# State products and scores in 64x32 tiles, w1 loaded by head pairs, and a new order of the work

## The chip, the core and the metric

The kernel runs on one core of one Trainium2 chip. The metric is the device time of one execution in microseconds (us), taken as the median of the runs. TensorE (PE) multiplies, with its weight loads shown apart (PEld); VectorE (DVE), ScalarE (ACT) and GpSimd (POOL) do the element work; SyncE (SP) issues most transfers (DMA).

## What is computed

Eight batches; in each, 512 rows of x in 8 heads of 64, and 32 state rows per head. Attention reads the state from x and x from the state; the 544 rows of 512 that result go through a normalized two-layer network with a hidden width of 2048.

```python
# B, H, S, Ns, D = 8, 8, 512, 32, 64
scores = x @ state^T / sqrt(D)                  # per batch and head
xread  = softmax(scores) @ state                # 512 rows
sread  = softmax(scores^T over x) @ x           # 32 rows
r   = concat([xread, sread], rows) -> (B, 544, 512)
rn  = (r - mean(r)) / sqrt(var(r) + 1e-6) * g_ln
out = r + relu(rn @ w_ch1) @ w_ch2              # w_ch1 512x2048, w_ch2 2048x512, both float64
```

## The kernel before

Numbers are held as a high and a low f16 part, and a product is made of three terms, high by high, high by low and low by high (`TERMS`). Heads are grouped as h = 4g + j, with g the half (0 or 1) and j the place in it (0 to 3); u is one of four units of 512 hidden columns, t, c and s are parts of the rows.

The weights come first. For each unit, `weights1` loads a float64 block of w1 in two transfers (L585), turns it to f32 on ACT and DVE (`words`), takes the column means off with f32 matmuls (L599), finds the largest value (L608), and splits the result into a high and a low part in the raw buffer. Four transfers inside SBUF (the last lines of `weights1`) then lay high and low of one head beside each other on the 128 partitions as `w1c`, so that one matmul with 128 rows makes two of the terms at once. `weights2` prepares w2 the same way without the rearrangement, and `sums_of_weights` makes the three weight sums that a Strassen form of the second product needs, by adding and subtracting 256-column blocks on PE with plus and minus the identity (L747).

Per batch, `attention` loads x and state, scales and splits them, transposes them by DMA, and computes the scores (L403): 32 state rows of one head against x, four heads side by side in 128x32 tiles of the PE array, 8 matmuls per g. After the softmax, `read_state` (L479) multiplies x by the numerators, and four f32 matmuls with a folded identity (L492) add the halves and turn the result. `state_products` (L665) multiplies each head's state rows by w1c, giving per unit and g a 128x512 block in a PSUM bank named `half`, with 8 matmuls in 128x32 tiles; ACT and DVE take it off as the high and low parts of `matrix`. Then `products` runs for each half batch and unit a first product (L799, from `matrix` and the softmax numerators `ea`) and a Strassen second product (L855, from `xs`, `w2h` and `sums`). Batch 0 has a plain form (L701 and L715). The state rows of all batches go through the network last (L808), with a second copy of the high halves of w1c, named `high`, that eight transfers make.

PSUM has 8 banks: four accumulators (`acc`), two `half`, and one pair named `banks`, which scores, read_state and the mix of L515 use in turn.

The order is written out by hand. Every step of every stream is a closure made by `do`; the text `PLAN` lists stream and step numbers, and `issue` calls them in this order. Each engine works through its own steps in that order, SP's transfers included, and a step waits for its inputs and for its buffer. `L186` is the line inside `do`, so nearly every element operation and transfer carries it and is told apart by its tiles.

## Time and profile before

| | |
|---|---|
| median of 3 runs | 668.11 us (667.76 to 668.94) |
| span of the profiled execution | 665.9 us |
| PE busy | 626.3 us (94%) |
| DVE busy | 498.0 us (75%) |
| ACT busy | 388.2 us (58%) |
| POOL busy | 216.7 us (33%) |
| bytes moved by DMA | 69.63 MB, mean 105 GB/s |

The span runs from the first to the last instruction of one profiled execution, whose own time is not given apart; the span lies 2.2 us below the median of the runs. A matmul's recorded duration is its latency: matmuls are pipelined, so what a row of n of them costs PE is read from the start of one row of the timeline to the start of the next.

### The profile page before, as it was taken

The page shows a single profiled execution, that of the slowest core. Times are in us where ns is not written, and L with a number is a line of the kernel's source. Part 1 is how long each engine was busy: PE and PEld are TensorE (multiplying, and loading weights), DVE is VectorE, ACT ScalarE, POOL GpSimd, SP SyncE. Part 2 cuts the span into 40 slices and gives each one's busy share as a digit, 9 for nine tenths or more (in the row PEclk, how much of TensorE's full clock was granted, in tenths as well). Part 3 has the DMA queues.
Part 4 walks back from the last instruction along what each step waited for, and adds up shares of the span by engine and source line. Part 5 has one row for each costly group of instructions (what it writes and reads, how often), then busy time and mean ns, then how long its engine had stood idle before and what let it go on. Part 6 is the DMA issues. An engine that isn't in the chain of part 4 may idle for free.

```text
span 665.9 us, 14680 instructions
## 1 busy us (share of the span) xinstructions
PE 626.3 (94%) x5948; PEld 493.1 (74%) x5948; DVE 498.0 (75%) x1002; ACT 388.2 (58%) x699; POOL 216.7 (33%) x189
## 2 busy tenths in 40 slices
PE   0676999999999999999999999999999999999996
PEld 0242755548887887788888888878778887888885
DVE  5989986697788677966887689777976897465533
ACT  5488989667546474547465756465546564344331
POOL 0000333321344325323452226433433343234222
PEclk9977999999999999999999999999999999999998
DMA  8999836924231534330516142305142311244221
GB/s 324 309 278 210 259 103 146 141 57 103 71 74 37 136 104 78 95 94 8 92 32 162 67 88 68 97 5 122 35 126 47 76 32 43 81 116 104 73 56 32
DMA packets 98563, 69.63 MB, mean 105 GB/s; under 512 B 72704, under 2 KB 90624, under 8 KB 98048
## 3 DMA queue, kind: packets, MB, share of 16 engines
q1 hardware_dynamic: 96384, 64.77, 37.5%
q0 software_dynamic: 864, 3.15, 2.6%
q8 instruction: 46, 0.75, 0.5%
q10 hardware_dynamic: 1248, 0.79, 0.4%
q14 instruction: 21, 0.17, 0.1%
HBM read 28.05 MB, written 9.44 MB: 56 GB/s over the span
## 4 chain that ended last, share of the span: by engine, by line
PE 90%; DVE 5%; DMA 2%; ACT 1%; issue 1%; DVEq 0%; SPq 0%
PE acc L855 41%; PE half L799 22%; PE acc L715 6%; PE half L665 5%; PE acc L701 3%; PE half L808 3%; PE acc L747 2%; PE acc L599 2%; PE banks L403 1%; DVE w_t L186 1%; PE banks L479 1%; PE banks L515 1%; PE banks L492 1%; DMA x_f<-in_x_dram 1%; PE acc L608 1%; DMA w1c<-raw 1%
## 5 line engine op out<-in xcount | busy, mean ns | idle before, releaser
L855 PEld LDWEIGHTS <-xs 128*128 128x128 f16 x2520 | 242.4, 98 | 43.6 <-issue 15.3
L186 POOL TENSOR_TENSOR xs<-rs,xs 128x512 f16<-128x512 f32 x120 | 142.4, 1199 | 272.7 <-ACT xs L186 207.1
L855 PE MATMUL acc<-w2h,xs 128*128 128x256 f16 x1440 | 183.0, 273 | 0.0
L799 PE MATMUL half<-ea,matrix 128*128 128x256 f16 x1344 | 159.4, 273 | 0.0
L799 PEld LDWEIGHTS <-matrix 128*128 128x128 f16 x1344 | 130.7, 98 | 16.6 <-issue 0.8
L855 PE MATMUL acc<-sums,xs 128*128 128x256 f16 x1080 | 141.9, 273 | 0.0
L186 DVE SCALAR_TENSOR_TENSOR rs<-half,rs 128x256 f32<-128x256 f32 x224 | 89.4, 419 | 27.6 <-ACT rs L186 13.3
L186 ACT ACTIVATE xs<-rs 128x512 f16<-128x512 f32 x128 | 77.1, 618 | 40.5 <-DVE rs L186 33.8
L186 ACT ACTIVATE xs<-half 128x256 f16<-128x256 f32 (+1 forms) x112 | 53.6, 487 | 72.5 <-PE half L799 50.5
L186 DVE SCALAR_TENSOR_TENSOR xs<-half,xs 128x256 f16<-128x256 f32 (+1 forms) x112 | 61.2, 550 | 28.1 <-ACT xs L186 24.5
L186 ACT ACTIVATE matrix<-half,hs 128x512 f16<-128x512 f32 x56 | 38.0, 687 | 35.2 <-PE half L665 34.9
L186 DVE SCALAR_TENSOR_TENSOR matrix<-half,hs,matrix 128x512 f16<-128x512 f32 x56 | 41.2, 742 | 16.0 <-ACT matrix L186 15.3
L186 ACT ACTIVATE rs<-half 128x256 f32<-128x256 f32 x56 | 21.3, 381 | 42.5 <-PE half L799 40.1
L715 PE MATMUL acc<-w2h,hid 128*128 128x512 f16 x192 | 43.1, 379 | 0.0
L186 DVE TENSOR_TENSOR strip<-acc,strip 128x256 f32<-128x256 f32 (+1 forms) x60 | 33.2, 554 | 10.5 <-PE acc L855 7.5
L665 PE MATMUL half<-w1c,sT 128*32 128x512 f16 x448 | 33.5, 384 | 1.9 <-DVE rs L186 1.0
L186 POOL TENSOR_TENSOR ts<-ts,mA 128x1024 f32<-128x1024 f32 (+1 forms) x8 | 14.4, 1804 | 60.9 <-DVE mA L186 54.5
L715 PEld LDWEIGHTS <-hid 128*128 128x128 f16 x192 | 18.5, 98 | 20.9 <-issue 0.4
L186 DVE SCALAR_TENSOR_TENSOR x<-x_f,x_s,x 128x512 f16<-128x512 f32 x32 | 24.8, 798 | 5.3 <-ACT x L186 5.3
L186 DVE BATCH_NORM_STATS2 s<-xr 128x6 f32<-128x512 f32 x32 | 21.6, 684 | 8.7 <-ACT xr L186 8.6
L186 ACT ACTIVATE x<-x_f,x_s 128x512 f16<-128x512 f32 x32 | 21.7, 713 | 9.8 <-DVE x_s L186 9.8
L186 POOL TENSOR_TENSOR hid<-strip,hid 128x512 f16<-128x512 f32 x16 | 18.5, 1170 | 26.6 <-ACT hid L186 26.5
(152 smaller groups left out, 770.1 us busy)
## 6 DMA issues: line engine op xcount, KB each, us to landing
raw<-in_moe_w_ch_dram SPq DMA_DIRECT2D x9, 1024.0 KB, 7.3
out_dram<-xr SPq DMA_DIRECT2D x16, 512.0 KB, 3.0
x_f<-in_x_dram SPq DMA_DIRECT2D x15, 512.0 KB, 5.6
sums<-in_moe_w_ch_dram SPq DMA_DIRECT2D x7, 1024.0 KB, 8.2
ek<-ea SPq DMA_DIRECT2D x56, 64.0 KB, 2.1
ek<-ek SPq DMA_DIRECT2D x7, 512.0 KB, 4.3
xr<-part POOLq DMA_DIRECT2D x6, 512.0 KB, 5.0
w1c<-raw SPq DMA_DIRECT2D x8, 256.0 KB, 5.1
```

The costliest lines, as they stand in the source:

```text
L186: return lambda: f(*map(now, args), **{k: now(v) for k, v in kw.items()})
L403: nc.tensor.matmul(o[32 * j:32 * j + 32], lhsT=sT[:, g, a, 32 * j:32 * j + 32], rhs=xT[:, s, 4 * g + j].rearrange("p c t -> p (c t)"), sta ...
L479: nc.tensor.matmul(ps_z[:, h // 4, :, h % 4], lhsT=xv[:, c // hc, h, c % hc], rhs=ebT[:, :, h // 4, c, 32 * (h % 4):32 * (h % 4) + 32], st ...
L492: nc.tensor.matmul(pr[:, g], lhsT=z4[:, g, i], rhs=fold, start=i == 0, stop=i == 1, skip_group_check=True)
L599: nc.tensor.matmul(ps, lhsT=gm[:, k:k + 1].broadcast_to([P, P]), rhs=t4[:, k], start=k == 0, stop=k == 3)
L665: nc.tensor.matmul(ps[32 * j:32 * j + 32], lhsT=sT[:, g, a, 32 * j:32 * j + 32], rhs=w[:, 2 * g + j // 2, j % 2], start=a == 0, stop=a == ...
L701: nc.tensor.matmul(o[:, 256 * f:256 * f + 256], lhsT=m[:, g, i, P * (q + f):P * (q + f) + P], rhs=ea[:, s, k, g], start=f == 0 and g == 0 ...
L715: nc.tensor.matmul(po, lhsT=hid[:, i, q, c * P:(c + 1) * P], rhs=w[:, j, q], start=first and q == 0 and n == 0, stop=last and q == 3 and n ...
L747: nc.tensor.matmul(o, lhsT=signs[:, k // 2], rhs=v[k], start=start and k == 0, stop=k == 3, skip_group_check=True)
L799: nc.tensor.matmul(ps[:, 256 * q:256 * q + 256], lhsT=m[:, h, i, P * (2 * k + q):P * (2 * k + q) + P], rhs=ea[:, 0, j, h, 256 * g:256 * g ...
L808: nc.tensor.matmul(ps[:, 256 * q:256 * q + 256].rearrange("p (t n) -> p t n", t=2), lhsT=w[:, k // 2, k % 2, fs] if k < H else wn[:, k - H ...
L855: nc.tensor.matmul(po[o], lhsT=y[:, n, i, o] if o < 2 else x[:, o - 2, n, i], rhs=v[j], start=u == 0 and n == 0 and k == 0 and o in (2, 1, ...
```

## The change

- **State products.** One step per unit makes both g. Each matmul has 64 rows and 32 columns of the array: g picks the upper or lower 64 rows, j the quarter of the columns. There are 24 per unit (three terms, four j, two g) where there were 16. From batch 1 on the results go to the two banks of `banks` and are taken off in one ACT and one DVE instruction of 2x512 columns; before, each g had its own `half` bank and its own pair of 512 columns.
- **Scores.** The same tiles: 24 matmuls in one step where two steps had 8 each.
- **w1.** It is loaded so that the partition is (g, row of the head) and the free index is (j, column), in four transfers per unit in place of two, and the split writes w1c directly. The 16 transfers of 256 KB inside SBUF and the eight that made `high` are gone. The gain vector and the state rows follow that layout, and L808 reads w1c alone with the same number of matmuls.
- **read_state.** The three terms apart: 48 matmuls of 64 columns where there were 32; the four f32 fold matmuls become one f32 transpose, after two copies of 64 rows, one on ACT and one on DVE.
- **Weight sums.** Full 512-column blocks; one bank is continued from sum to sum: 12 matmuls of 512 columns per unit where there were 32 of 256.
- **Batch 0** loads x in two halves by rows (pieces of 512 bytes) where it had halves by heads (1 KB).
- **Order.** `PLAN` is replaced as a whole:

```diff
-    "1:0 1:3-4 1:1-2 1:5-12 4:1 1:19 1:72 0:0 4:6 1:20 1:24-25 4:5 4:7 4:0 4:3 1:17-18 4:2 4:4 3:1 3:6 1:22-23 "
+    "0:0 1:1 1:0 1:2-3 1:5 1:4 1:6-8 4:1 1:9-11 1:71 1:12 1:18 1:21 4:6 1:19 1:22 1:13 4:0 1:16 1:23 1:17 2:0 4:3 "
...
+            o, i = (xf[:, hh], src[:, :, 2 * hh:2 * hh + 2]) if b == 0 else (xf[:, 0, hs], src[:, hs])
+            yield do(engines[hh].dma_start, out=o, in_=i)
...
-        def scores(s, g, o, sT, xT):
-            for a in range(2):
+        def scores(s, ps, sT, xT):
+            for n, (a, i) in enumerate(TERMS):
                 for j in range(4):
-                    nc.tensor.matmul(o[32 * j:32 * j + 32], lhsT=sT[:, g, a, 32 * j:32 * j + 32],
-                                     rhs=xT[:, s, 4 * g + j].rearrange("p c t -> p (c t)"),
-                                     start=a == 0, stop=a == 1, skip_group_check=True)
-
-        psv = ps if parts == 1 else ps.rearrange("p s (g t) -> p g s t", g=G)
-        eB = quad("eB").rearrange("p (g s t) -> p g s t", g=G, s=parts)
+                    for g in range(G):
+                        k = hc * (4 * s + j)
+                        nc.tensor.matmul(ps[32 * j:32 * j + 32, g, w * s:w * s + w],
+                                         lhsT=sT[D * g:D * g + D, a, 32 * j:32 * j + 32],
+                                         rhs=xT[D * g:D * g + D, k:k + hc, i], start=n == 0, stop=n == 2,
+                                         skip_group_check=True)
...
         def read_state(ps_z, x16, ebT):
-            xv = x16.rearrange("p (s h c) i d -> p s h c (i d)", s=parts, c=hc)
-            for h in range(H):
+            for j in range(4):
                 for c in range(C):
-                    nc.tensor.matmul(ps_z[:, h // 4, :, h % 4], lhsT=xv[:, c // hc, h, c % hc],
-                                     rhs=ebT[:, :, h // 4, c, 32 * (h % 4):32 * (h % 4) + 32],
-                                     start=c == 0, stop=c == C - 1, skip_group_check=True)
+                    a = hc * (4 * (c // hc) + j) + c % hc
+                    for n, (i, k) in enumerate(TERMS):
+                        nc.tensor.matmul(ps_z[:, j], lhsT=x16[:, a, i], rhs=ebT[:, k, :, c, 32 * j:32 * j + 32],
+                                         start=c == 0 and n == 0, stop=c == C - 1 and n == 2, skip_group_check=True)
         yield do(read_state, ps_z, x16, ebT)
-        z = halves("z").bitcast(F32)[:, 0:512]
-        z4 = z.rearrange("p (g i n) -> p g i n", g=G, i=2)
-        pr = pz[:, 1, 0:G * D].rearrange("p (g d) -> p g d", g=G)
+        z = halves("z").bitcast(F32)[:, 0:P]
+        pr = pz[:, 1, 0:G * D]
         sread = fixed([P, G, D], F32, "sread")
-        yield do(nc.scalar.activation, z, pz[:, 0], AF.Copy)
-
-        def fold_halves(pr, z4):
-            for g in range(G):
-                for i in range(2):
-                    nc.tensor.matmul(pr[:, g], lhsT=z4[:, g, i], rhs=fold, start=i == 0, stop=i == 1,
-                                     skip_group_check=True)
-        yield do(fold_halves, pr, z4)
-        yield do(nc.vector.tensor_tensor, sread, pr, rB.unsqueeze(2).broadcast_to([P, G, D]), ALU.mult)
+        for g, copy in enumerate((partial(nc.scalar.activation, func=AF.Copy), nc.vector.tensor_copy)):
+            r = slice(D * g, D * g + D)
+            yield do(copy, z[r].rearrange("p (j n) -> p j n", j=4), ps_z[r, :, g])
+        yield do(nc.tensor.transpose, pr, z, idf)
+        yield do(nc.vector.tensor_tensor, sread, pr.rearrange("p (g d) -> p g d", g=G),
+                 rB.unsqueeze(2).broadcast_to([P, G, D]), ALU.mult)
...
+            rows_of = w1[:, 1024 * u:1024 * u + 1024].rearrange("(g j d) f -> g d j f", g=G, j=4)
+            for k in range(2):
+                nc.sync.dma_start(out=raw[:, 1024 * k:1024 * k + 1024], in_=rows_of[:, :, 2 * fh + k])
...
-        hl = raws[1].bitcast(F16).rearrange("p (i e) -> p i e", i=2)
-        yield from split(hl[:, 0], hl[:, 1], t, scale)
-        hl = hl.rearrange("p i (k f) -> p i k f", k=4)
-        w = narrow(u, "w1c").bitcast(F16).rearrange("p (k s f) -> p k s f", k=4, s=2)
-        w1c[u] = w
-        for i in range(2):
-            for s in range(2):
-                to = 64 * (i ^ s)
-                yield do(nc.sync.dma_start, out=w[to:to + 64, :, s], in_=hl[64 * s:64 * s + 64, i])
+        w = narrow(u, "w1c").bitcast(F16).rearrange("p (i e) -> p i e", i=2)
+        yield from split(w[:, 0], w[:, 1], t, scale)
+        w1c[u] = w.rearrange("p i (j f) -> p i j f", j=4)
...
-        def multiply(ps, g, sT, w):
-            for a in range(2):
+        def multiply(ps0, ps1, sT, w):
+            for n, (a, i) in enumerate(TERMS):
                 for j in range(4):
-                    nc.tensor.matmul(ps[32 * j:32 * j + 32], lhsT=sT[:, g, a, 32 * j:32 * j + 32],
-                                     rhs=w[:, 2 * g + j // 2, j % 2], start=a == 0, stop=a == 1, skip_group_check=True)
+                    for g in range(G):
+                        nc.tensor.matmul((ps0, ps1)[g][32 * j:32 * j + 32],
+                                         lhsT=sT[D * g:D * g + D, a, 32 * j:32 * j + 32],
+                                         rhs=w[D * g:D * g + D, i, j], start=n == 0, stop=n == 2, skip_group_check=True)
         sT = results[b][1]
         for u in range(U):
             m = matrix[b][u] = block(4, f"matrix_{u}", 1, "matrix").bitcast(F16).rearrange("p (g i f) -> p g i f", g=G, i=2)
-            for g in range(G):
-                ps = accumulator() if b == 0 else half()
-                scale = CM if b == 0 else hs[:, u:u + 1]
-                yield do(multiply, ps, g, sT, w1c[u])
-                yield do(nc.scalar.activation, m[:, g, 0], ps, AF.Copy, scale=scale)
-                yield do(nc.vector.scalar_tensor_tensor, m[:, g, 1], ps, scale, m[:, g, 0], ALU.mult, ALU.subtract)
+            scale = CM if b == 0 else hs[:, u:u + 1]
+            if b == 0:
+                ps = [accumulator() for _ in range(G)]
+                todo = [(ps[g], m[:, g, 0], m[:, g, 1]) for g in range(G)]
+            else:
+                two = banks()
+                ps = [two[:, g] for g in range(G)]
+                todo = [(two, m[:, :, 0], m[:, :, 1])]
+            yield do(multiply, *ps, sT, w1c[u])
+            for v, hi, lo in todo:
+                yield do(nc.scalar.activation, hi, v, AF.Copy, scale=scale)
+                yield do(nc.vector.scalar_tensor_tensor, lo, v, scale, hi, ALU.mult, ALU.subtract)
...
+        def add(sign, first, last, ps, *v):
+            for i in range(2):
+                nc.tensor.matmul(ps, lhsT=signs[:, sign], rhs=v[i], start=first and i == 0, stop=last and i == 1,
                                  skip_group_check=True)
-        for n in range(2):
-            ps = [accumulator() for _ in range(2)]
-            (b21, b22), (b11, b12) = ([[w[:, i, n, k, 256 * x:256 * x + 256] for i in range(2)] for x in range(2)]
-                                      for k in range(2))
-            t3, t2, n4 = ([sums16[:, u, k, i, n] for i in range(2)] for k in range(3))
-            o = [v[:, 256 * x:256 * x + 256] for v in ps for x in range(2)]
-            for pairs in (((t3, b22, b12), (b12, b12, b11)), ((t2, b22, b12),), ((n4, b21, t2),)):
-                first = len(o)
-                def subtract_all(*v, first=first):
-                    for k in range(len(v) // 5):
-                        subtract(first != 1 and k == 0, *v[5 * k:5 * k + 5])
-                todo = [(d, a, b, o.pop(0)) for d, a, b in pairs]
-                yield do(subtract_all, *[v for d, a, b, p in todo for v in (p, *a, *b)])
-                for d, a, b, p in todo:
-                    yield do(nc.scalar.activation, d[0], p, AF.Copy)
-                    yield do(nc.vector.tensor_tensor, d[1], p, d[0], ALU.subtract)
+        def difference(ps, a0, a1, b0, b1):
+            add(0, True, False, ps, a0, a1)
+            add(1, False, True, ps, b0, b1)
+        (b21, b22), (b11, b12) = ([[w[:, i, :, k, 256 * x:256 * x + 256] for i in range(2)] for x in range(2)]
+                                  for k in range(2))
+        t3, t2, n4 = ([sums16[:, u, k, i] for i in range(2)] for k in range(3))
+        ps, pb = (accumulator().rearrange("p (n e) -> p n e", n=2) for _ in range(2))
+        yield do(difference, ps, *b22, *b12)
+        yield do(nc.scalar.activation, t3[0], ps, AF.Copy)
+        yield do(nc.vector.tensor_tensor, t3[1], ps, t3[0], ALU.subtract)
+        yield do(difference, pb, *b12, *b11)
+        yield do(add, 0, False, True, ps, *b11)
+        yield do(nc.scalar.activation, t2[0], ps, AF.Copy)
+        yield do(nc.vector.tensor_tensor, t2[1], ps, t2[0], ALU.subtract)
+        yield do(nc.scalar.activation, b12[0], pb, AF.Copy)
+        yield do(nc.vector.tensor_tensor, b12[1], pb, b12[0], ALU.subtract)
+        yield do(add, 1, False, True, ps, *b21)
+        yield do(nc.scalar.activation, n4[0], ps, AF.Copy, scale=-1.0)
+        yield do(nc.vector.scalar_tensor_tensor, n4[1], ps, -1.0, n4[0], ALU.mult, ALU.subtract)```

What the new order does is seen in the engines' rows. First SP's queue in the first 90 us, where the rearranging transfers stood (x_f and s_j are loads of a batch, ebT a transpose). Before:

```order
L186 DMA_TRANSPOSE ebT<-eb 128x16x128
L626 DMA raw<-in_moe_w_ch_dram 128x2x1024
L186 DMA w1c<-raw 64x4x512 x2
L186 DMA w1c<-sums 64x4x512
L186 DMA w1c<-raw 64x4x512 x6
L626 DMA raw<-in_moe_w_ch_dram 128x2x1024
L186 DMA w1c<-sums 64x4x512 x3
L186 DMA s_j<-in_state_dram 128x2x64
L626 DMA sums<-in_moe_w_ch_dram 128x2x1024
```

The same place with the change:

```order
L191 DMA x_f<-in_x_dram 128x4x256
L616 DMA raw<-in_moe_w_ch_dram 128x2x1024
L191 DMA_TRANSPOSE ebT<-eb 128x16x128
L616 DMA raw<-in_moe_w_ch_dram 128x2x1024
L191 DMA s_r<-in_state_dram 32x8x64
L191 DMA s_j<-in_state_dram 128x2x64
```

The loads of w2 (L626, now L616) follow one another with no w1c transfer between them.

Second, DVE in the same stretch, from the end of the first unit's w1 (its low part is written to `raw` before, to `w1c` now) to the first blocks of `matrix`. Before:

```order
L186 SCALAR_TENSOR_TENSOR raw<-w_t,of_weights,raw 128x2048 x2
L186 SCALAR_TENSOR_TENSOR w_t<-w_t,gx,acc 128x512 x4
L186 TENSOR_REDUCE dA<-ts 128x16
L186 TENSOR_SCALAR dA<-dA 128x16
L186 SCALAR_TENSOR_TENSOR sums<-w_t,of_weights,sums 128x2048
L186 RECIPROCAL dA<-dA 128x16
L186 SCALAR_TENSOR_TENSOR matrix<-acc,matrix 128x512
```

With the change:

```order
L191 STREAM_TRANSPOSE ef<-ts 128x512
L191 TENSOR_SCALAR of_weights<-of_weights 128x1
L191 SCALAR_TENSOR_TENSOR matrix<-acc,matrix 128x512
L191 TENSOR_SCALAR is_297<-of_weights 128x1
L191 RECIPROCAL of_weights<-is_297 128x1
L191 SCALAR_TENSOR_TENSOR w_t<-w_t,gx,acc 128x512
L191 SCALAR_TENSOR_TENSOR ea<-ef,ea 128x512
```

The first block of `matrix` now comes after the low part of one unit of w1, where three units' low parts stood ahead of it; the other units' follow later.

Third, DVE in the middle of the program, where a batch's state products are taken off between steps of the hidden blocks (`rs`, `xs`). Before:

```order
L186 SCALAR_TENSOR_TENSOR eb<-eB,eb 128x1024
L186 SCALAR_TENSOR_TENSOR matrix<-half,hs,matrix 128x512
L186 SCALAR_TENSOR_TENSOR xs<-half,xs 128x2x256
L186 TENSOR_REDUCE dA<-ts 128x32
L186 TENSOR_SCALAR dA<-dA 128x32
L186 RECIPROCAL dA<-dA 128x32
L186 SCALAR_TENSOR_TENSOR matrix<-half,hs,matrix 128x512 x2
```

With the change:

```order
L191 SCALAR_TENSOR_TENSOR ea<-ef,ea 128x1024
L191 SCALAR_TENSOR_TENSOR matrix<-banks,hs,matrix 128x2x512
L191 SCALAR_TENSOR_TENSOR xs<-half,xs 128x2x256
L191 SCALAR_TENSOR_TENSOR rs<-half,rs 128x256 x4
L191 SCALAR_TENSOR_TENSOR xs<-half,xs 128x2x128 x2
L191 SCALAR_TENSOR_TENSOR rs<-half,rs 128x256
L191 SCALAR_TENSOR_TENSOR matrix<-banks,hs,matrix 128x2x512
```

There are half as many take-offs, each of 2x512 columns, and other steps stand between them.

More of the change, by code (lines that the diff above doesn't have):

```diff
@@ L1 @@
 from contextlib import ExitStack
+from functools import partial
 import concourse.bass as bass
@@ L281, in load_batch @@
         engines = nc.sync, nc.sync if b > 0 else nc.scalar
-        xf = rows("x_f").rearrange("p (h c d) -> p h c d", h=H, c=C)
+        parts = 2 if b == 0 else 1
+        xf = rows("x_f").rearrange("p (s h c d) -> p s h c d", s=parts, h=H, c=C // parts)
         sj = fixed([P, G, D], F32, "s_j")
@@ L887, in products @@
             yield together()
-    high, state_rows_T = [None] * U, [None]
-    def high_halves(u):
-        high[u] = quad("high").bitcast(F16).rearrange("p (k f) -> p k f", k=4)
-        for s in range(2):
-            half = slice(64 * s, 64 * s + 64)
-            yield do(nc.sync.dma_start, out=high[u][half], in_=w1c[u][half, :, s])
+    state_rows_T = [None]
     def state_rows():
@@ L937, in moe_attention @@
         streams += these
-    streams += [list(state_rows()), *(list(high_halves(u)) for u in range(U))]
+    streams += [list(state_rows())]
     streams += [list(s) for s in products(B)]
```

108 lines of the change are left out of this document (50 added, 58 removed), and 242 rows, old and new, of the table PLAN.

## The prediction, made before the change was run

> **What bounds the kernel now.** I read the busy times by stage first, then what PE waited for after the start, then the chain that ended last. Columns of the first view: stretch, its length, busy time of each engine with its instructions, granted TensorE clock, DMA share, GB/s.
>
> ```profile
> core 0: us, PE busy (x) PEld busy (x) DVE busy (x) ACT busy (x) POOL busy (x), PEclk, DMA share, GB/s
> 0.00:81.00 81.00, 49.12 (x373) 27.06 (x373) 68.42 (x127) 57.53 (x80) 7.34 (x12) 0.87 0.93 274
> 81.00:660.00 579.00, 577.12 (x5583) 465.99 (x5575) 427.51 (x873) 330.68 (x620) 209.37 (x177) 1.00 0.34 81
> ```
> ```profile
> PE half L665 <- DVE rs L186: 1.0, 1, 1.0
> PE half L665 <- DVE xs L186: 0.9, 1, 0.9
> ```
> ```profile
> PE 90%; DVE 5%; DMA 2%; ACT 1%; issue 1%; DVEq 0%; SPq 0%
> ```
>
> From 81 to 660 us PE is busy 577 of 579 us at full clock, and its two waits there come to 1.9 us. DVE, the next engine, is busy 427.5 of 579 (74%). So after the start a microsecond of PE work is a microsecond of time, and work taken from DVE, ACT or DMA alone is worth nothing. Before 81 us DVE leads (68.4 of 81).
>
> **Prices on PE.** Counts of the parts that change, then rows of the timeline; the cost of a row is the distance to the next start.
>
> ```profile
> L665 PE MATMUL half<-w1c,sT 128*32 128x512 f16 x448 | 33.5, 384 | 1.9 <-DVE rs L186 1.0 <-DVE xs L186 0.9
> L403 PE MATMUL banks<-xT,sT 128*32 128x512 f16 x112 | 8.0, 382 | 0.0
> L479 PE MATMUL banks<-ebT,x 128*128 128x64 f16 x256 | 9.5, 199 | 0.0
> L492 PE MATMUL banks<-fold,z 128*128 128x64 f32 x64 | 8.2, 272 | 0.7 <-ACT z L186 0.7
> L747 PE MATMUL acc<-w2h,signs 128*128 128x256 f16 x112 | 15.4, 273 | 0.0
> L747 PE MATMUL acc<-sums,signs 128*128 128x256 f16 x16 | 3.1, 272 | 0.0
> ```
> ```profile
> 202.28 0.82 PE L855 MATMUL acc<-w2h,xs 128*128 128x256 f16 x6
> 203.03 0.62 PE L665 MATMUL half<-w1c,sT 128*32 128x512 f16 x8
> 203.58 1.48 PE L855 MATMUL acc<-w2h,xs 128*128 128x256 f16 x12
> 204.90 0.82 PE L855 MATMUL acc<-sums,xs 128*128 128x256 f16 x6
> ...
> 86.50 1.05 PE L665 MATMUL half<-w1c,sT 128*32 128x512 f16 x16
> 87.48 1.49 PE L701 MATMUL acc<-ea,matrix 128*128 128x256 f16 x12
> ...
> 140.64 7.93 PE L715 MATMUL acc<-w2h,hid 128*128 128x512 f16 x36
> 148.41 1.47 PE L747 MATMUL acc<-w2h,signs 128*128 128x256 f16 x12
> ...
> 157.36 1.10 PE L479 MATMUL banks<-ebT,x 128*128 128x64 f16 x32
> 158.29 1.47 PE L799 MATMUL half<-ea,matrix 128*128 128x256 f16 x12
> 159.60 1.00 PE L492 MATMUL banks<-fold,z 128*128 128x64 f32 x8
> 160.44 0.38 PE L747 MATMUL acc<-w2h,signs 128*128 128x256 f16 x2
> ...
> 241.64 0.27 PE L186 MATMUL banks<-idf,x_am 128*2 128x128 f32 x1
> 241.75 0.82 PE L855 MATMUL acc<-sums,xs 128*128 128x256 f16 x6
> ```
>
> A 256-column matmul costs 0.109 us (158.29 to 159.60, 12 of them); one of 512 columns 0.216 (140.64 to 148.41, 36). A group of 8 in 128x32 tiles begins 0.09 after the six before it are through (202.28 + 6 x 0.109 = 202.94, start 203.03) and holds PE 0.55: two waves of 0.216 and 0.12 more. So a lone group of 8 costs 0.64, and a group of 16 costs 0.98 + 0.09 = 1.07. How such a wave runs is seen in slices of 20 ns (the number in brackets after PE is how many matmuls are in flight, after PEld how many weight loads):
>
> ```profile
> 274.72:274.74 0.02, 0.02 (x4) 0.02 (x7) 0.02 (x1) 0.00 (x0) 0.00 (x0) 1.00 0.00 0
> 274.80:274.82 0.02, 0.02 (x4) 0.02 (x7) 0.02 (x1) 0.00 (x0) 0.00 (x0) 1.00 0.00 0
> 274.84:274.86 0.02, 0.02 (x4) 0.00 (x0) 0.02 (x2) 0.00 (x0) 0.00 (x0) 1.00 0.00 0
> 274.94:274.96 0.02, 0.02 (x8) 0.00 (x0) 0.02 (x1) 0.00 (x0) 0.00 (x0) 1.00 0.37 90
> ```
>
> Four matmuls start together, one per quarter; the weights of the next four are loaded by 274.84, under the first four; the next four start at 274.93, a streaming time later.
>
> **State products.** The changed group has 24 matmuls in eight tiles: three waves, if the two row halves run together, 0.09 + 3 x 0.216 + 0.12 = 0.86. Bound above, if the halves take turns: six waves, 1.51. No row shows two halves of 64 rows at once. The nearest is the 32-row tiles of L530:
>
> ```profile
> 43.52 0.96 PE L530 MATMUL acc<-sh,ea 32*128 32x64 f16 x34 [1.01 <-DVE ea L186]
> ```
>
> 34 of them start within about 0.76 us (0.96 less one latency, 0.20 as L479's row has it), 0.022 each, while 64 columns on the whole array cost 0.029 (0.93/32, 157.36 to 158.29). Calls on different row strips follow one another there, so strips do overlap somewhat. I take 0.86. By the Trainium skill, "TensorEngine Tiling (Array Packing)", section Tiling Modes, tiles operate independently and a change of mode drains the array; by it too the group has three waves, and the 0.09 and 0.12 above are such drains.
>
> Counting PE's rows from the first second product (L715) on, before has 46 lone groups of 8 and 5 of 16: 46 x 0.64 + 5 x 1.07 = 34.8 us. The change has 29 groups: 29 x 0.86 = 24.9. **Gain 9.9.** Scores there: 8 lone groups and 3 of 16, 8.3, against 7 groups, 6.0: **gain 2.3.**
>
> **Weight sums.** 128 x 0.109 = 14.0 against 48 x 0.216 = 10.4: **gain 3.6.** **read_state**, seven batches: 48 for 32 matmuls, 16 x 0.029 x 7: **loss 3.2.** **The fold**: 0.84 a batch (159.60 to 160.44), against one f32 transpose. A transpose with a two-column weight costs 0.11; a full f32 weight costs about as much to load again (the fold's eight records are 0.105 apart with only 64 columns each). I take 0.21, between 0.11 and 0.42: 7 x 0.63, **gain 4.4** (2.9 to 5.1). One more group of 12 of L701 stands ahead of L715: **gain 1.3.** Sum of the dense part: 9.9 + 2.3 + 3.6 - 3.2 + 4.4 + 1.3 = 18.3 us.
>
> **The shared bank pair.** State products now use `banks`. Its take-off has no row of 2x512 columns from PSUM with both parts; the nearest are
>
> ```profile
> L186 ACT ACTIVATE xr<-banks,ux 128x1024 f32<-128x1024 f32 x14 | 15.6, 1111 | 6.0 <-PE banks L515 5.3 <-DMA s_r<-in_state_dram 0.5
> L186 DVE SCALAR_TENSOR_TENSOR eb<-eB,eb 128x1024 f16<-128x1024 f32 x8 | 10.5, 1310 | 1.5 <-ACT eb L186 1.5
> ```
>
> 1.11 + 1.31 = 2.4 us, behind whatever stands in the two queues. In PE's new rows the next user of the pair mostly stands 3 to 13 us of PE work later, but three times 2.6 (24 matmuls of 256 columns). Bounds: nothing, or 2 us at each of the eight places under 4 us, 16. I take 0.5: three short waits. What is behind such a wait is all of PE.
>
> **The start.** The chain of waits held the rearranging transfers, and DVE's timeline shows what went on meanwhile:
>
> ```profile
> 49.62 2.27 DVE raw L186
> 52.55 5.25 DMA w1c<-raw
> 57.85 1.90 PE acc L665 x16
> ...
> 83.98 2.59 PE acc L715 x12
> ```
> ```profile
> 6.39 0.69 DVE L186 TENSOR_REDUCE x_part<-x_f 128x1 f32<-128x512 f32 x1 [4.55 <-DMA x_f<-in_x_dram]
> ...
> 59.92 0.63 DVE L186 SCALAR_TENSOR_TENSOR matrix<-acc,matrix 128x512 f16<-128x512 f32 x1
> ...
> 80.62 1.27 DVE L186 SCALAR_TENSOR_TENSOR w2h<-w_t,of_weights,w2h 128x1024 f16<-128x1024 f32 x1
> ```
>
> The first state products no longer wait 5.25 us for w1c, and DVE has two units' low parts less ahead of the first `matrix`. But the dense stretch begins with L715, which needs the first w2h; its DVE step ended at 81.9. Adding up DVE's rows ahead of that step with the durations of the trace I get about 71 us before and 72 with the change, and PE has about the same work ahead of L715 (29 against 28 us). So the saved transfers are hidden by DVE: taken at 0. If DVE had gaps that they caused (it is idle 12.6 of the first 81 us, 4.55 of it for the first load) it gains up to 5. The smaller pieces of batch 0's x can cost up to 2, late for everything. The range of this term is -5 to +3. SP loses 24 issues and gets 8 of w1 more; nobody waits for SP in the dense part.
>
> **Sum.** 665.9 - 18.3 + 0.5 = 648.1 us of span; the median of the runs lies 2.2 above the span: **650 us.**
>
> **The rivals.**
> *Row halves take turns* (slower). Each of 36 groups costs 1.51: 43.8 + 10.6 against 34.8 + 8.3, a loss of 11.3, less the other gains of 6.1: 5.2 us worse than now, 673. It decides from 1.37 us per group, where 36 groups eat all gains. Against it: quarters do run at once, and L530's spacing.
> *Weight loads come out of cover.* Each wave of eight needs eight loads into tiles still in use; if they wait, each group pays two of the 0.14 us that the eight loads in the slices took: 36 x 0.28 = 10 us, 660. The slices speak against it: the loads of the second four ran under the first four in the same rows. By the Trainium skill, "TensorE: Matmul & The Clock Gate", Part 3, The mechanism, loads overlap matmuls in flight only where their row group differs; that rule would give this rival, and the slices of this trace disagree with it.
> *The bank pair stalls PE.* 0.4 us at each of 28 take-offs: 11 us, 661. For it: one pair now serves nine uses a batch; against it: the spacing above.
> *The fourth unit of w1 comes late.* Its low part stands after 83 us of DVE work, after 63 before. Its first products have about 4 us to spare on PE. If DVE's queue slips by 10, PE waits 6: 656.
>
> **How the numbers follow.** Likeliest case 0.68, 650, own range 643 to 655; halves in turn 0.06; loads 0.08; bank pair 0.10; fourth unit 0.08. The range from 641 takes in a start that is 5 us better with a cheap transpose, and to 662 the loads, the bank pair and the fourth unit; it leaves out the slower case and mixtures. About 0.2% (1.3 us) is what a measurement of this kernel tells from no change. Faster 0.91, same 0.03 (two of the losing cases at once), slower 0.06.
>
> **What would show it.** A state group on PE that holds it about 0.86 with eight matmuls in flight per wave; L747's successor at 0.216 a matmul; the z transpose near 0.2; PE over 99% busy after the first L715's successor, which starts near 82 us; few waits of PE on ACT or DVE `matrix` at `banks`. Wrong, if a group takes over 1.2 us, if PE shows gaps ahead of `banks`, or if the dense part starts later than 87 us.

## The result: 793.45 us, slower by 19%

The changed kernel takes 793.45 us (793.14 to 794.35 in 4 runs) against 667.93 us (667.28 to 668.94) for the kernel before: a ratio of 1.188, 95% interval 1.1865 to 1.1899. The forecast was 650 us. The span of the profiled execution is 791.9 us, 126.0 more than the 665.9 of before.

The stages come first, with the columns of the prediction's first view:

```profile
0.00:54.00 54.00, 4.71 (x7) 1.75 (x7) 8.40 (x22) 8.07 (x14) 0.70 (x6) 1.00 0.20 67
54.00:86.00 32.00, 5.10 (x8) 2.01 (x8) 3.23 (x4) 1.18 (x1) 0.00 (x0) 0.88 0.13 52
...
218.00:785.00 567.00, 560.42 (x5825) 452.74 (x5825) 412.26 (x830) 314.10 (x575) 209.85 (x174) 1.00 0.33 78
```

In the first 86 us no engine of the core does anything for long: PE is busy for 9.8 us, DVE for 11.6. What runs is DMA, and it runs at a crawl: a share of 0.13 of the 16 engines, which is two of them, and 52 GB/s. Before, the first 81 us had a share of 0.93 and 274 GB/s. The dense part is healthy: 560.4 us of PE work in 567.

SyncE's own timeline shows what the crawl is (start, length of the issue, line, kind, transfer, count):

```profile
1.93 21.26 SPq L583 DMA_DIRECT2D sums<-in_moe_w_ch_dram  x4
23.23 80.11 SPq L583 DMA_DIRECT2D raw<-in_moe_w_ch_dram  x8
103.46 23.51 SPq L191 DMA_TRANSPOSE xT<-x  x1
127.08 1.17 SPq L191 DMA_TRANSPOSE sT<-sh  x1
128.30 1.09 SPq L583 DMA_DIRECT2D raw<-in_moe_w_ch_dram  x2
129.49 21.62 SPq L191 DMA_TRANSPOSE xT<-x  x1
```

Eight w1 transfers of 512 KB hold SP for 80.11 us, 10.0 each, and 512 KB in 10.0 us is 52 GB/s again. Everything on SP queues behind them: the transpose of batch 0's x is issued at 103.46. SP's timeline of the kernel before has it at 15.19:

```profile
15.19 4.88 SPq L186 DMA_TRANSPOSE xT<-x  x1
```

PE's waits in the changed kernel (waited for, total, times, longest) name both:

```profile
PE acc L595 <- DVE w_t L191: 118.6, 7, 35.3
PE banks L406 <- DMA xT<-x: 19.3, 1, 19.3
```

and so does the chain that ended last, in which PE has fallen from 90% to 53%, with SP's queue and DMA at 25% together:

```profile
PE 53%; DVE 15%; SPq 13%; DMA 12%; ACT 4%; issue 2%; DVEq 0%; POOL 0%; ACTq 0%
```

The first wait is put down to DVE, but DVE was busy for 11.6 of 86 us: it waits for the loads in its turn, as its own waits up to 218 us show:

```profile
DVE raw L191 <- DMA raw<-in_moe_w_ch_dram: 82.3, 5, 17.6
DVE sums L191 <- DMA sums<-in_moe_w_ch_dram: 45.9, 3, 17.2
```

The first second product starts at 218.1 us where it started at 83.8, 134.3 later. From there to the end it takes 573.8 us against 582.1, 8.3 less. The two make up the 126.0.

The prices that the prediction put on the new groups of matmuls can be read directly (start, busy time, then the form and the count; a cost is the distance to the next start):

```profile
263.99 1.03 PE L745 MATMUL acc<-w2h,signs 128*128 128x512 f16 x4
264.95 0.84 PE L656 MATMUL banks<-w1c,sT 64*32 64x512 f16 x24
265.72 0.82 PE L713 MATMUL acc<-w2h,hid 128*128 128x512 f16 x3
...
274.56 0.33 PE L191 MATMUL banks<-idf,z 128*128 128x128 f32 x1
274.73 1.15 PE L745 MATMUL acc<-w2h,signs 128*128 128x512 f16 x4
```

A state group holds PE for 0.77 us, and it begins 0.10 after the four matmuls ahead of it are through (263.99 + 4 x 0.216 = 264.85): 0.87, where 0.86 was forecast. The transpose of z costs 0.17, where 0.21 was forecast.

### The profile page after: what moved, and what is told of

Its sections match the earlier page's. It is cut to its first block, busy times and chain, and to the rows that moved or that the text cites. A ratio compares the mean times of both kernels' runs of the same rounds, so it can differ in the third digit from the quotient of the medians.

```text
span 791.9 us, 15186 instructions
## 1 busy us (share of the span) xinstructions
PE 620.6 (78%) x6268; PEld 484.0 (61%) x6268; DVE 484.6 (61%) x958; ACT 371.9 (47%) x655; POOL 221.3 (28%) x189
## 4 chain that ended last, share of the span: by engine, by line
PE 53%; DVE 15%; SPq 13%; DMA 12%; ACT 4%; issue 2%; DVEq 0%; POOL 0%; ACTq 0%
PE acc L858 25%; PE half L800 15%; SPq L583 12%; DMA raw<-in_moe_w_ch_dram 7%; PE acc L713 4%; DMA sums<-in_moe_w_ch_dram 4%; DVE rs L191 3%; PE half L810 2%; PE banks L656 2%; DVE xs L191 1%; PE acc L745 1%; SPq L191 1%; DVE strip L191 1%; DVE matrix L191 1%; PE banks L480 1%
## 5 line engine op out<-in xcount | busy, mean ns | idle before, releaser
L191 POOL TENSOR_TENSOR xs<-rs,xs 128x512 f16<-128x512 f32 x120 | 144.8, 1220 | 287.6 <-ACT xs L191 206.4
L800 PE MATMUL half<-ea,matrix 128*128 128x256 f16 x1344 | 162.2, 273 | 1.4 <-DVE xs L191 0.9
L595 PE MATMUL acc<-w_t,gm 128*128 128x512 f32 x32 | 27.2, 1008 | 118.6 <-DVE w_t L191 118.6
L191 DVE SCALAR_TENSOR_TENSOR rs<-half,rs 128x256 f32<-128x256 f32 x224 | 90.9, 418 | 47.7 <-ACT rs L191 29.4
L191 ACT ACTIVATE xs<-rs 128x512 f16<-128x512 f32 (+1 forms) x128 | 76.3, 618 | 52.9 <-DVE rs L191 46.7
L191 ACT ACTIVATE xs<-half 128x256 f16<-128x256 f32 (+1 forms) x112 | 53.3, 486 | 85.2 <-PE half L800 33.9
L595 PEld LDWEIGHTS acc<-w_t,gm 128*128 128x128 f32 x32 | 9.1, 310 | 134.5 <-DVE w_t L191 126.0
L191 DVE SCALAR_TENSOR_TENSOR xs<-half,xs 128x256 f16<-128x256 f32 (+1 forms) x112 | 60.8, 548 | 17.4 <-ACT xs L191 17.2
L191 POOL TENSOR_TENSOR ts<-ts,mA 128x1024 f32<-128x1024 f32 (+1 forms) x8 | 14.4, 1806 | 168.4 <-DVE mA L191 165.5
L191 DVE TENSOR_SCALAR raw<-raw 128x1024 uint32<-128x1024 uint32 x9 | 6.2, 697 | 82.3 <-DMA raw<-in_moe_w_ch_dram 82.3
L191 ACT ACTIVATE raw<-raw 128x1024 f32<-128x1024 f32 x9 | 10.4, 1157 | 91.8 <-DMA raw<-in_moe_w_ch_dram 91.8
L713 PE MATMUL acc<-w2h,hid 128*128 128x512 f16 x192 | 43.4, 379 | 1.0 <-DVE w2h L191 0.5
L191 DVE SCALAR_TENSOR_TENSOR matrix<-banks,hs,matrix 128x1024 f16<-128x1024 f32 x28 | 35.6, 1271 | 7.7 <-ACT matrix L191 7.7
L191 ACT ACTIVATE matrix<-banks,hs 128x1024 f16<-128x1024 f32 x28 | 31.1, 1110 | 17.9 <-PE banks L656 17.3
L191 DVE TENSOR_TENSOR strip<-acc,strip 128x256 f32<-128x256 f32 (+1 forms) x60 | 33.1, 552 | 8.3 <-PE acc L858 5.8
L191 ACT ACTIVATE rs<-half 128x256 f32<-128x256 f32 x56 | 21.3, 380 | 29.7 <-PE half L800 23.2
L191 ACT ACTIVATE sums<-sums 128x1024 f32<-128x1024 f32 (+1 forms) x8 | 9.8, 1244 | 49.2 <-DMA sums<-in_moe_w_ch_dram 49.2
L191 DVE TENSOR_SCALAR sums<-sums 128x1024 uint32<-128x1024 uint32 x7 | 4.8, 691 | 45.9 <-DMA sums<-in_moe_w_ch_dram 45.9
```

The lines of the kernel that those rows point to most:

```text
L191: return lambda: f(*map(now, args), **{k: now(v) for k, v in kw.items()})
L595: nc.tensor.matmul(ps, lhsT=gm[:, k:k + 1].broadcast_to([P, P]), rhs=t4[:, k], start=k == 0, stop=k == 3)
L713: nc.tensor.matmul(po, lhsT=hid[:, i, q, c * P:(c + 1) * P], rhs=w[:, j, q], start=first and q == 0 and n == 0, stop=last and q == 3 and n ...
L800: nc.tensor.matmul(ps[:, 256 * q:256 * q + 256], lhsT=m[:, h, i, P * (2 * k + q):P * (2 * k + q) + P], rhs=ea[:, 0, j, h, 256 * g:256 * g ...
```

## The experiments

Two questions: whether the pattern of the w1 loads is the whole of the loss, and why the dense part gained 8 us instead of 18.

**w1 by half.** The changed kernel addresses a w1 transfer as [g][row of the head][column], with g, of size 2, outermost. The experiment makes two transfers by g, each with the 64 rows outermost. The bytes, the pieces of 4 KB and the number of transfers stay.

```diff
-            for k in range(2):
-                nc.sync.dma_start(out=raw[:, 1024 * k:1024 * k + 1024], in_=rows_of[:, :, 2 * fh + k])
+            for g in range(G):
+                nc.sync.dma_start(out=raw[D * g:D * g + D].rearrange("d (j f) -> d j f", j=2),
+                                  in_=rows_of[g][:, 2 * fh:2 * fh + 2])
```

> The change with one edit: each w1 transfer takes one head half g, with its 64 rows as the outermost index and two heads j behind it, where it took both halves with g (2) outermost. Bytes (512 KB), pieces (4 KB) and the number of transfers (four a unit) stay. Theory A (a transfer is spread over as many DMA engines as its outermost index allows, so two): w1 arrives at the rate of before, the DMA share of the first 140 us goes from 0.13 to above 0.6, the first second product starts near 85 us in place of 218, time 655 to 662. Theory B (the slowness is in the new row pattern or in the doubled number of transfers): still above 750. On the rest: by the prediction's sum 650; by the dense part of the profile of the change (573 us from the first second product to the end, 582 before) 660.

Measured: 668.49 us (666.88 to 672.12), 1.0017 of before, 0.9996 to 1.0039. These two code lines are worth 125 us. By the Trainium skill, "DMA: Bandwidth & Descriptors", section "Why a DMA increments its semaphore by 16 and not by 1", a transfer is spread over the largest number of engines up to 16 that divides the slowest dimension of both sides; a slowest dimension of 2 gives two engines. The trace agrees: a share of 0.13 with 2 outermost, of 1.05 with 64.

But the kernel is no faster than before, and slower than the 655 to 662 that theory A expected. The start is still 8.9 us late (first second product at 92.7). One reason is the rate of the loads. The first row is of this kernel, the second of the one with neighbouring heads below, whose transfers fill 128 partitions:

```profile
10.00:20.00 10.00, 0.92 (x3) 0.57 (x3) 4.65 (x14) 2.17 (x5) 0.00 (x0) 1.00 1.05 226
```
```profile
10.00:20.00 10.00, 3.56 (x6) 1.95 (x7) 9.01 (x18) 7.12 (x9) 0.00 (x0) 1.00 1.02 410
```

All engines are taken in both, and the transfers to 64 partitions move 226 GB/s against 410. By the Trainium skill, "SBUF — State Buffer", section "Door 1: The DMA port swizzle", partitions 0 to 63 reach only 8 of the 16 ports by which DMA enters, and so do 64 to 127; the ratio of 0.55 agrees with that, though no run here separates the ports from other effects of a half transfer. SP's queue, and x's transpose in it, waits accordingly:

```profile
7.79 9.43 SPq L583 DMA_DIRECT2D raw<-in_moe_w_ch_dram  x8
20.88 14.19 SPq L191 DMA_TRANSPOSE xT<-x  x1
```

The transpose is both longer and later than before (15.19 and 4.88 us long). That it is later has another reason, the gains. Their two transfers land late, and `gm`, which scales them, stands first on DVE, so the maxima of x behind it, and with them the transpose, wait too:

```profile
13.80 0.17 DVE L191 TENSOR_SCALAR gm<-gx 128x4 f32<-128x4 f32 x1 [12.09 <-DMA gx<-in_moe_g_ln_dram]
13.88 1.27 DVE L191 TENSOR_REDUCE x_part<-x_f 128x1 f32<-128x512 f32 x2
```

Why the gains land this late no run shows. From the first second product to the end this kernel takes 574.2 us, 7.9 less than before.

**Halves in turn.** The w1-by-half kernel with the twelve matmuls of the upper 64 rows issued ahead of the twelve of the lower ones.

```diff
-            for n, (a, i) in enumerate(TERMS):
-                for j in range(4):
-                    for g in range(G):
+            for g in range(G):
+                for n, (a, i) in enumerate(TERMS):
+                    for j in range(4):
```

> As e1_w1_by_half, and in state products the loop over g stands outside: the three waves of one half of the rows, then those of the other. If the two row halves run together as the prediction priced it, a group of 24 goes from 0.86 us to about 1.29 to 1.51 (five or six waves), 31 groups: 13 to 20 us slower than e1_w1_by_half. If the halves never ran together, no difference.

Measured: 671.21 us (668.83 to 674.66), 1.0053 of before (1.0032 to 1.0073): 2.7 more than with the halves mixed, and not 13 to 20. The expectation fell, and a row says why:

```profile
240.21 0.87 PE L657 MATMUL banks<-w1c,sT 64*32 64x512 f16 x24
241.01 1.16 PE L859 MATMUL acc<-sums,xs 128*128 128x256 f16 x9
```

The group holds PE for 0.80 us against 0.77. Six waves of 512 columns in turn would be 6 x 0.216 = 1.30. So the two row halves run at once even where their matmuls are issued one half after the other. A slice 0.09 us into the group has eight matmuls in flight, where one half alone would have four:

```profile
240.30:240.32 0.02, 0.02 (x8) 0.02 (x14) 0.02 (x2) 0.00 (x0) 0.00 (x0) 1.00 0.00 0
```

**State products twice.** The w1-by-half kernel computes every state product twice.

```diff
-            for n, (a, i) in enumerate(TERMS):
+            for n, (a, i) in (*enumerate(TERMS), *enumerate(TERMS)):
```

> As e1_w1_by_half, and every state product is computed twice into the same bank (same result). If PE bounds the dense part, 32 groups get three waves of 0.216 more: 18 to 21 us slower than e1_w1_by_half. If other waits bound it, clearly less.

Measured: 682.50 us (682.11 to 683.1), 1.0225 of before (1.0204 to 1.0245): 14.0 more. On PE a group costs 1.42 against 0.77:

```profile
135.86 1.49 PE L657 MATMUL banks<-w1c,sT 64*32 64x512 f16 x48
137.28 1.90 PE L714 MATMUL acc<-w2h,hid 128*128 128x512 f16 x8
```

In the dense part, 28 groups x 0.65 = 18.2 us of work were added and 13.9 came out (588.1 us from the first second product to the end, against 574.2); the groups of batch 0 added nothing. The other 4.3 went into time in which PE had been waiting: idle PE in the dense part falls from 7.0 us (560.3 busy of 567.3) to 3.8 (577.4 of 581.2), its longest single wait, for the transfer of ek, from 2.6 to 0.7, and about 1 us more is idle time hidden behind the modelled ends of the matmuls. So the faster dense part holds 7 us in which PE has nothing to do, and the doubling could use some 4 of them.

**Neighbouring heads.** If a pair is heads 2j and 2j + 1 instead of j and j + 4, its rows of w1 are 128 neighbouring rows. One transfer per half unit then fills 128 partitions, as in the kernel before. The gains, too, take one transfer where the change has two by half. Everything on PE stays; the state rows take four transfers by pair.

```diff
-            for k in range(2):
-                nc.sync.dma_start(out=raw[:, 1024 * k:1024 * k + 1024], in_=rows_of[:, :, 2 * fh + k])
+            nc.sync.dma_start(out=raw.rearrange("p (k f) -> p k f", k=2),
+                              in_=w1[256 * fh:256 * fh + 256, 1024 * u:1024 * u + 1024].rearrange("(k p) f -> p k f", p=P))
...
-            v = xf[:, k, 4 * g:4 * g + 4] if parts == 2 else xf[:, 0, 4 * g + 2 * k:4 * g + 2 * k + 2]
+            v = xf[:, k, g::2] if parts == 2 else xf[:, 0, 4 * k + g:4 * k + g + 3:2]
...
-                                         lhsT=ek[:, h // 4, h % 4, (2 * t + c) * P:(2 * t + c + 1) * P],
+                                         lhsT=ek[:, h % 2, h // 2, (2 * t + c) * P:(2 * t + c + 1) * P],
```

> The changed kernel with the head pairs chosen differently: a pair is two neighbouring heads (2j and 2j+1) instead of heads j and j+4. The rows of w1 that belong to a pair are then 128 neighbouring rows, so w1 and the gains load as in the kernel before, one transfer of 128 partitions per half unit and one for the gains; the states load in four transfers by pair instead of one. All products, tiles, places in PSUM and the order of the instructions stay those of the changed kernel. Theory (the loads' pattern is the whole of what the change lost at the start): the first second product starts at 84 to 88 us as in the kernel before (83.8), and from there it takes the 574 us that the changed kernel with its w1 loads cut by half took (574.2), so 659 to 664 us in all, 0.987 of before. Rival 1 (the dense part itself was held back by what the slow start left behind, such as the queue on SP): the dense part shortens too, to 568 us or less, and the time is 655 or less. Rival 2 (the start's order, not the loads, is what makes it late, through the gains' step that stands first on VectorE): the first second product stays at 91 us or later, 667 us or more.

Measured: 655.56 us (654.99 to 655.86), 0.9819 of before (0.9804 to 0.9833). It beats both kernels. In its profile the first second product starts at 80.6 us, 3.2 earlier than before, and 573.1 us follow, 9.0 less than before. The theory's two numbers were 84 to 88 and 574, so the start came out better than it expected, and rival 1's 568 is excluded: the loads, of w1 and of the gains together, were the whole loss of the start. `gm` now starts at 7.33 instead of 13.80, and x's transpose at 14.57 and 7.87 us long instead of 20.88 and 14.19. So of the 12.1 us that the start gained on w1 by half, these rows put about 6 on the earlier gains and 6 on the faster queue; no run changes only one of the two.

**The gain step later.** In all versions of the change so far, DVE's first step with an input is `gm`, which waits for the transfer of the gains. Here it goes back behind the first scales of x.

```diff
-    "0:0 1:1 1:0 1:2-3 1:5 1:4 1:6-8 4:1 1:9-11 1:71 1:12 1:18 1:21 4:6 1:19 1:22 1:13 4:0 1:16 1:23 1:17 2:0 4:3 "
+    "1:1 1:0 1:2-3 1:5 1:4 1:6-8 4:1 1:9-11 1:71 0:0 1:12 1:18 1:21 4:6 1:19 1:22 1:13 4:0 1:16 1:23 1:17 2:0 4:3 "
```

> The kernel with neighbouring heads and one thing more: the step that scales the gains (one VectorE instruction that waits for their transfer) stands behind the first maxima and scales of x, as in the kernel before, instead of ahead of everything on VectorE. Theory (VectorE's first maxima of x wait behind it): the maximum of x goes back to about 8 us (15.75 with the loads cut by half, 8.28 before), and 1 to 5 us come off the start and off the time against the same kernel with the step in front; the first second product starts at about 84. Rival (VectorE's work on w1, or the loads of w1, set the start, and the maxima of x have slack): less than 0.5 us difference.

Measured: 656.76 us (655.66 to 658.26), 0.9845 of before (0.9825 to 0.9866), so nothing gained, and the theory falls. The wait only changes its name. First with `gm` in front, then with `gm` behind:

```profile
7.33 0.17 DVE L191 TENSOR_SCALAR gm<-gx 128x4 f32<-128x4 f32 x1 [5.62 <-DMA gx<-in_moe_g_ln_dram]
7.41 1.27 DVE L191 TENSOR_REDUCE x_part<-x_f 128x1 f32<-128x512 f32 x2
```
```profile
6.79 0.69 DVE L191 TENSOR_REDUCE x_part<-x_f 128x1 f32<-128x512 f32 x1 [5.08 <-DMA x_f<-in_x_dram]
8.08 0.69 DVE L191 TENSOR_REDUCE x_part<-x_f 128x1 f32<-128x512 f32 x1 [0.60 <-DMA x_f<-in_x_dram]
```

The last maximum of x ends at 8.7 us in the one and at 8.8 in the other: with the gains out of the way DVE waits for x itself, whose second half lets the last maximum start only at 8.08.

**More work for DVE and ACT.** Three kernels, to see how much room the element engines have in the dense part: the kernel with neighbouring heads with the low parts of `matrix` computed twice (DVE), the same with the high parts twice (ACT), and the kernel before with its low parts twice (DVE), all in batches 1 to 7.

```diff
-                yield do(nc.vector.scalar_tensor_tensor, lo, v, scale, hi, ALU.mult, ALU.subtract)
+                def low(*args):
+                    for _ in range(2 if b > 0 else 1):
+                        nc.vector.scalar_tensor_tensor(*args)
+                yield do(low, lo, v, scale, hi, ALU.mult, ALU.subtract)
```

> The kernel with neighbouring heads, in which VectorE computes the low parts of the state products (matrix) twice in batches 1 to 7: 28 steps of 1.27 us, 35.6 us more of VectorE work, the same result. The question is where the dense part's expected gain went: 18.3 us expected, 9.0 measured (573.1 us from the first second product to the end, against 582.1), while PE's named waits there rose from 1.9 to 6.3 us, most of them for VectorE. Theory (with its shorter row PE now runs up against VectorE's queue, and that is where a part of the gain went): the time rises by 4 to 15 us, and PE's named waits after 80 us by as much. Rival 1 (the few waits are accidents of the order, and VectorE at 74% has slack): less than 1.5 us. Rival 2 (it is the length of the chain through ScalarE and VectorE and not VectorE's queue): about as much here as where ScalarE's step is doubled.

> The kernel with neighbouring heads, in which ScalarE computes the high parts of matrix twice in batches 1 to 7: 28 steps of 1.11 us, 31 us more of ScalarE work, the same result. Theory (VectorE's queue is what PE runs up against, ScalarE at 57% is not): the time rises by less than a third of what doubling VectorE's step gives, 0 to 4 us. Rival (the chain's length through both): as much as for VectorE's step, in proportion to 1.11 and 1.27 us.

> The kernel before, in which VectorE computes the low parts of the state products twice in batches 1 to 7: 56 steps of 0.74 us, 41.6 us more of VectorE work, the same result. Theory (before, PE's longer row left VectorE more room): the time rises by less than half of what the same doubling gives in the kernel with neighbouring heads, though more work is added. Rival (VectorE's room was the same before, at 75% busy): the rise is the same or larger, in proportion 41.6 to 35.6.

| kernel | added | time | of before (95%) | rise |
|---|---|---|---|---|
| neighbouring heads, low parts twice | DVE 35.6 us | 676.73 | 1.0134 (1.0105 to 1.0163) | 17 to 21 |
| neighbouring heads, high parts twice | ACT 31 us | 671.35 | 1.0051 (1.0034 to 1.0067) | 12 to 16 |
| before, low parts twice | DVE 41.6 us | 678.61 | 1.0161 (1.0139 to 1.0183) | 10.8 |

The rise of the first two is given against the two measurements of the kernel with neighbouring heads, 655.56 above and 659.2 below; from the first second product to the end the profiles give 20, 16 and 9. The 17 to 21 are more than the 4 to 15 expected, and the 12 to 16 more than the 0 to 4. The 10.8 are just over half of the first rise, where under half was expected, and far from the rival's equal rise. For each us of DVE work, 0.26 us come out in the kernel before and about twice that with neighbouring heads. ACT's work, with a busy share of only 57%, costs 0.4 to 0.5 for each us against 0.5 to 0.6 for DVE's, which fits the rival on the length of the chain; the theory that it is DVE's queue alone falls. The run doesn't separate the two altogether: a longer ACT step also holds up what stands behind `matrix` on DVE, and there PE waits 4.5 us for `matrix` and 3.2 for `xs`. PE's waits show where it goes (low parts twice, neighbouring heads; waited for, total, times, longest):

```profile
PE banks L657 <- DVE matrix L677: 7.5, 7, 1.6
PE banks L513 <- DVE matrix L677: 2.6, 2, 1.3
...
PE banks L482 <- DVE matrix L677: 2.3, 4, 1.2
...
PE banks L408 <- DVE matrix L677: 1.6, 2, 1.1
```

14.0 us in 15 waits, all for the bank pair that `matrix` must leave. Without the doubling such waits come to 0.4 us. So the pair, which every state product from batch 1 on now goes through, is often free just in time: a take-off that is longer by 1.27 us puts it on the path in 15 places. In the kernel before, which has two `half` banks for it, the same doubling shows 3.8 us at L802, the product that shares those banks.

**Less work for DVE.** The kernel with neighbouring heads, with less DVE work in batches 1 to 7. The maxima and sums of the softmax read half their columns and so do the statistics, so these values are not the reference's.

```diff
-            yield do(nc.vector.tensor_reduce, m_, t3, AX.X, ALU.max)
+            n = 32 if b == 0 else 16
+            yield do(nc.vector.tensor_reduce, m_, t3[:, :, 0:n], AX.X, ALU.max)
...
-            yield do(nc.vector.bn_stats, s6, v)
+            yield do(nc.vector.bn_stats, s6, v[:, 0:n_cols])
```

> The kernel with neighbouring heads, in which VectorE does less in batches 1 to 7: the maxima and sums of the softmax over the states read 16 of 32 columns, the maxima of the other softmax 256 of 512, and the statistics 256 of 512 columns, so these values are not the reference's (about 3.2 us a batch less, 22 us in all); every other instruction stays. Theory (what is left of the expected gain sits in PE's short waits for VectorE, 7 us beside the one wait for the ek transfer): the time falls by 3 to 8 us. Rival (the waits are for the length of single chains or for ScalarE and transfers, and VectorE's queue only matters when it gets more work): less than 1.5 us.

Measured: 655.79 us (655.37 to 657.1), 0.9829 of before (0.9807 to 0.9851), no change. Its profile, though, had a late start: the first second product at 84.5 us, and 570.8 us from there. So both kernels ran again, side by side.

> The kernel with neighbouring heads once more, in more runs and beside the next kernel: the first comparison of the two (655.56 and 655.79) mixes the dense part with a start that took 80.6 us in one profiled execution and 84.5 in the other, at mean granted clocks of 0.989 and 0.981. Expected: 655 to 658, and 0.980 to 0.986 of before.

> The kernel with neighbouring heads and 22 us less VectorE work in batches 1 to 7, once more, beside the one with all of it. Theory (VectorE's queue holds back a part of the dense stretch): 1.5 to 4 us less than the kernel beside it, as its dense part was 2.3 us shorter in the profile (570.8 against 573.1 us from the first second product to the end). Rival (VectorE's queue only matters when it gets more work): within 1 us of it.

Measured: 659.2 us (657.56 to 659.67), 0.9874 of before (0.9856 to 0.9892), for the kernel with neighbouring heads, and 654.55 us (653.0 to 659.27), 0.9816 (0.9786 to 0.9847), with less DVE work. The first lies outside the 655 to 658 that were expected. So the gain of that kernel is 1.3 to 1.8%. The medians over both sittings are 657.6 (9 runs) and 655.6 (10 runs): 22 us less of DVE's work are worth about 2 us, between no gain and 4.7 in the two sittings, and the dense parts of the four profiles agree with a small effect (573.1 and 574.0 against 570.8 and 573.2). That is neither the 3 to 8 of the theory nor the rival's nothing; it leaves most of PE's waits standing.

What varies most from execution to execution is the start, together with PE's granted clock. The stretch from 44 to 64 us of the kernel with neighbouring heads, in the profile with the first second product at 80.6 us and in the one with it at 83.4:

```profile
44.00:64.00 20.00, 16.81 (x193) 10.49 (x194) 19.63 (x33) 18.00 (x25) 1.05 (x1) 0.79 0.54 125
```
```profile
44.00:64.00 20.00, 16.29 (x165) 9.81 (x166) 19.56 (x35) 16.51 (x22) 1.05 (x1) 0.67 0.49 122
```

At 0.67 for 0.79, 28 fewer matmuls are recorded in 20 us. Which of the two, clock or work, leads is not shown.

## Why the prediction was wrong

**The step that failed is the start**, "taken at 0" with a range of -5 to +3. It cost +134.3 us. The prediction counted the transfers ("SP loses 24 issues and gets 8 of w1 more") and added up DVE's rows, but gave the loads of w1 no term of their own. It did not look at how the new ones are addressed: [2][64][1024], with the 2 outermost. The number of transfers and their bytes were right; the rate was the error, 52 GB/s where 387 (before) and 410 (neighbouring heads) were moved from 10 to 20 us. 125 us of it went with that outermost 2, and the remaining 8.9 with the loads into 64 partitions and the late gains. The reasoning that DVE hides the start held only while the loads kept ahead of DVE. And "nobody waits for SP" was said of the dense part, whereas in the start x's transposes stand on SP behind the w1 transfers. With the loads spread as before (neighbouring heads) the start came out at -3.2 and -0.4 in the two profiles, inside the range. Of the prediction's own signs of being wrong one showed: the dense part started later than 87 us.

None of the rivals held this. The fourth, that w1's fourth unit comes late, had the right place and a price of 6 us, for DVE's work and not for the transfers.

**The dense part was right in its work and wrong in its sum.** Adding up, for each line, the distances from each row of PE's timeline to the next start, from the first second product to the end (before 83.8 to 665.9, neighbouring heads 80.6 to 653.7; sums can differ by 0.1 through rounding):

| us of PE | before | neighbouring heads | gain | forecast |
|---|---|---|---|---|
| state products | 29.8 | 23.1 | 6.7, and 2.0 for 22 fewer entries of 0.09 on the rows ahead: 8.7 | 9.9 |
| scores | 7.2 | 5.4 | 1.8, and 0.4 for 4 fewer entries: 2.2 | 2.3 |
| weight sums | 14.7 | 12.8, with 1.9 of the wait for ek | 3.8 without it | 3.6 |
| read_state | 6.9 | 9.9 | -3.0 | -3.2 |
| fold, now z's transpose | 6.1 | 0.8 | 5.3 | 4.4 |
| L701's successor | 9.3 | 8.1 | 1.2 | 1.3 |
| sum of these | | | 18.2 | 18.3 |
| the four large products, which did not change | 476.9 | 481.0 | -4.1, or -6.5 with the 2.4 of the entries | 0 |
| the wait for ek | | | -1.9 | 0 |
| the rest | | | -0.7 | 0 |
| in all | 582.1 | 573.1 | 9.0 | 18.3 |

Every price was good to about 1 us. The wrong sentence is "after the start a microsecond of PE work is a microsecond of time". It was read off a trace in which PE waited for 1.9 us, and it holds at the margin of that trace; taking 18 us off PE moved the margin. Some of PE's waits after the start show it:

```profile
PE banks L513 <- DMA ek<-ek: 1.7, 1, 1.7
PE half L801 <- DVE xs L191: 0.9, 2, 0.5
PE banks L191 <- DVE x_am L191: 0.5, 2, 0.3
PE acc L714 <- DVE w2h L191: 0.5, 1, 0.5
...
PE banks L657 <- DVE matrix L191: 0.4, 2, 0.2
```

and the stretches of the dense part, first of the kernel before, then with neighbouring heads:

```profile
83.80:660.00 576.20, 574.32 (x5553) 463.64 (x5551) 424.76 (x871) 328.25 (x616) 207.96 (x176) 1.00 0.33 80
```
```profile
80.60:648.00 567.40, 560.71 (x5828) 452.92 (x5827) 412.76 (x831) 314.25 (x574) 209.78 (x174) 1.00 0.33 78
```

PE is idle for 6.7 us where it was idle for 1.9. The other 4 us or so don't show as idle time. A pause costs more than the idle time that the profile gives, because the modelled end of the last matmul runs over into it:

```profile
259.44 0.82 PE L859 MATMUL acc<-sums,xs 128*128 128x256 f16 x6
260.80 1.47 PE L801 MATMUL half<-ea,matrix 128*128 128x256 f16 x12 [0.55 <-DVE xs L191]
```

The six matmuls are through at 259.44 + 6 x 0.109 = 260.09, and PE stands still for 0.71 us where 0.55 is given. The profile names 14 such waits behind the first second product; 0.16 us on each make up to 2.2 us, and pauses too short to be named the rest. That PE has room there is shown by the doubled state products, of which 4.3 us did not come out.

Eleven of the 14 waits are for a step of DVE. In ten of these the step had started right behind the one before it on DVE (no idle time is shown ahead of it), and in one it had waited for ACT. The bank pair's `matrix` makes up only 0.4 us. So the place of these steps in DVE's queue is the nearer suspect, not the bank pair. That is not proven: taking 22 us of other work off DVE gave only about 2 us, and no run changed the order of the steps.

**Rivals.** "Row halves take turns" is refuted twice, by the 0.77 us of a group and by the 0.80 with the halves issued one after the other. "Weight loads come out of cover" would have made the group 1.14 us; the group's 0.87 excludes that. The rule of the Trainium skill that was weighed there ("TensorE: Matmul & The Clock Gate", Part 3, The mechanism) disagrees with this row too. "The bank pair stalls PE" was 0.4 us and not 11, but the doubled low parts show that it was only about 1 us of take-off away. The shared pair's own term was forecast at 0.5.

## What to carry to other kernels

Read the address pattern of every changed transfer, above all the size of its outermost dimension and how many partitions it fills, before you count transfers and bytes: here that made 125 us, and choosing which rows form a pair so that they are neighbours brought it back and more. When a change takes work from an engine that is busy for 99% of a stretch, the part that comes out is bounded by what the next engines can do: look for the other engines' room at each hand-over, here half of it came out. Adding work to a suspected engine, and to the same engine in the kernel before, measures that room cheaply, but the answer for less work can be much smaller than the one for more.

## What the runs showed of the hardware that was not expected

- A transfer whose outermost dimension is 2 ran on two engines' worth of share (0.13) at 52 GB/s; the same bytes with 64 outermost took all of them, and the core moved 226 GB/s, into 64 partitions at a time; with transfers to 128 partitions it moved 410.
- Matmuls of the two 64-row halves ran at once even when one half's twelve were issued after the other's: eight were in flight 0.09 us into the group, and it took 0.80 us against 0.77 with the halves mixed.
- The granted clock in the start (0.67 or 0.79 from 44 to 64 us, same kernel) went with 2.8 us of difference in when the dense part began.
